# A fifth pair of row blocks by Winograd's seven products in the second GEMM of an H3 + feed-forward kernel

## The chip, the core and the metric

The kernel runs on one core of one Trainium2 chip. The metric is the device time of one execution in microseconds. TensorE (PE) multiplies matrices, VectorE (DVE) and ScalarE (ACT) work on elements, GpSimd (POOL) issues accumulating DMAs here, and SyncE (SP) issues all other DMAs from one queue, in order. Each engine runs its own instructions in the order in which they were written, and waits on semaphores for the others.

## The reference

With `xn = layernorm(q)` the output is the sum of three parts:

```
h   = silu(xn @ w1)                  # 2048 x 1024 @ 1024 x 3584
ffn = h @ w2                         # 2048 x 3584 @ 3584 x 1024
kv  = causal_conv4(k) * v
y   = long_conv(kv, ssm_k) + kv * ssm_D   # per channel, over 2048 steps
out = q + xn * y + ffn
```

All data is float32. Every matrix product is made of three fp16 matmuls (high x high, high x low, low x high), so that it keeps nearly float32's precision. To split a tile into its high and low part takes one ACT copy and one DVE subtraction.

## The kernel before, in words

**GEMM1** (`units`, `product`, `steps`) computes `h` transposed, in 14 pairs of 128 columns of `w1`. Most of it uses Winograd's form of Strassen's scheme: seven products of half-size blocks for eight. The names of the scheme are `A11, A12, A22, S1` to `S4` for sums of the left blocks and `B11, B21, B22, T1` to `T4` for those of the right; `PRODUCTS` lists the seven products P1, P7, P6, P2, P5, P3, P4 in the order in which they run. Each result goes through SiLU, is split, and is stored in DRAM: as four plain blocks a pair (`blocks`, tensor `hs`), or, for the pairs listed in `PAIRS`, as the seven left factors that GEMM2 wants (`quad`, tensors `hsf`). `quad` makes four sums on DVE (helper line 348) and seven half-size splits (lines 359 on ACT, 351 on DVE) where `blocks` makes two full-size splits for each of two row quarters.

**GEMM2** has two parts. The *plain* part (in `feed_forward`, matmuls in `steps2`, lines 1179 to 1181) runs over two halves of the output columns, 16 blocks of 128 rows and `NC` = 5 chunks of four column blocks of `h`. In the second half the last three row blocks run together, chunk by chunk, so that the places of w2's chunks come free one after the other. The *product* part (`units2`) covers the pairs in `PAIRS` (8, 9, 12, 13) for both halves at once: eight tiles, each of seven products, each product four steps of three matmuls, one step for each pair. P1 of the next tile runs between P5 and P3 of a tile. TensorE runs these in order; a step waits for its left factor (flag `h2`) and for its right factor (flag `w2f`).

**The factors of w2** are made by one generator, `norms_w2`, in a fixed order: ten plain chunks, then the seven factors in the order of `PRODUCTS`. Each waits for its place, one of eight SBUF tiles `x0` to `x7` (`places`): `W2PLACE` for the chunks, `FPLACE` for the factors. The raw blocks come from `load_w2`, which loads ahead as long as it finds a free buffer in `wraw` (two halves) or, once GEMM1 is over and two whole tiles of it are free, in `hf` (three tiles of two halves, which the evacuations use too). The sums T3, T2 and T4 build on one another and are held in place 6 (`hold`).

**The convolution** runs beside all this from about 180 us on, in eight groups of 128 channels: `gate` multiplies into the accumulator `acc` (one tile; a group's tile is free again when `signal_parts` has split all four parts of it into `cm` or `ht`), `stage1` transforms on TensorE (lines 1668 to 1670, tile `ps`), `transforms` does the rest on DVE in one chain through the tiles `spec` and `tmp`, `stage1_inv` goes back on TensorE (lines 1861 to 1863), `gated` writes `yt`, and POOL adds it to the output in DRAM. The buffers `hl` of a group's parts come free when its `stage1` is done; the next group's `gate` needs them.

**The order of the work** is written out by a planner, `Order`. Every part above is a Python generator; the planner always takes the operation that can start first by its own costs, less a bias of its stream, and emits it. So the order on each engine is fixed before the run. `yield r.ready` holds a whole generator, and everything behind it in the same generator, until the ring `r` has a free buffer.

**The last tile** of the product part doesn't add to the output by POOL but loads what is there (flag `conv out`: the convolution's last blocks for it must be on their way) and stores the sum, so its evacuation stands behind the convolution.

Of the kernel before, what the change touches and what calls it, by code (L numbers as in the profile page):

```python
# [20 lines left out]
P = 128  # L21
# [9 lines left out]
W = 512  # L31
# [20 lines left out]
RAWS = {"B11": [(0, 0)], "B21": [(1, 0)], "B22": [(1, 1)], "T1": [(0, 1), (0, 0)], "T2": [(0, 0)],  # L52
        "T3": [(1, 1), (0, 1)], "T4": [(1, 0)]}

# [241 lines left out]
def h3_ffn_kernel(ctx, tc, x, kp, vs, fs, shift, dskip, w1, w2, cfwd, cinv, out):  # L296
# [80 lines left out]
    dram = ctx.enter_context(tc.tile_pool(name="dram", bufs=1, space=bass.MemoryType.DRAM))  # L377
    hsf = [{p[0]: dram.tile([4, P, NQ, 2, P], F16, name=f"hsf{p[0]}{b}") for p in PRODUCTS.values()} for b in range(2)]
    hs = [dram.tile([4, P, NF, 2, P], F16, name=f"hs{b}") for b in range(4)]
# [528 lines left out]
    def quad(i, sp):  # L908

        def factors(names, hf, toks=()):  # L910
            n = len(names)
            yield hts.ready if n == 1 else hts.pairs
            ht, ttok = (hts.tile if n == 1 else hts.pair)([P, 4 * n, 2, P], F16, n)
            yield from split(ht[:, :, 0], ht[:, :, 1], hf, wsc[:, i, 2:3], toks)
            for f, name in enumerate(names):
                yield L(hsf[sp][name][:, :, PAIRS.index(i)].rearrange("q p h s -> p q (h s)"),
                        ht[:, 4 * f:4 * f + 4].rearrange("p q h s -> p q (h s)"))
# [216 lines left out]
    def feed_forward():  # L1134
# [12 lines left out]
        for h in range(2):  # L1147
            for ts in TOGETHER[h]:
                pos = {}
                for c in range(NC):  # L1150
                    for t in ts:
# [6 lines left out]
                        wc, wtok = w2c[h, c]  # L1158
                        yield from steps2(pos[t][0], hx, wc, c == 0, c == NC - 1)
                        htok.set()  # L1160
# [12 lines left out]

    def steps2(po, hx, wc, first, last, more=False, of=range(4), q=slice(0, W)):
        o = po[:, q]
        for n in of:
            def mm(n=n):
                kw = dict(skip_group_check=more)
                nc.tensor.matmul(o, hx[:, n, 0, :], wc[:, n, 0, q], start=first and n == 0, stop=False, **kw)  # L1179
                nc.tensor.matmul(o, hx[:, n, 0, :], wc[:, n, 1, q], start=False, stop=False, **kw)  # L1180
                nc.tensor.matmul(o, hx[:, n, 1, :], wc[:, n, 0, q], start=False, stop=last and n == 3, **kw)  # L1181
            yield T(mm, o, [hx[:, n], wc[:, n, :, q]], 3 * (size(o) / 2400 + 0.005))

# [13 lines left out]
    def units2():  # L1197

        def product2(n, u, o, first=False, of=range(4), q=slice(0, W)):
# [5 lines left out]
            if 3 not in of or q.stop < W:  # L1205
                return
            htok.set()
            if u == len(tiles2) - 1:
                wtok.set()
# [4 lines left out]
        for u in range(len(tiles2)):  # L1214
# [18 lines left out]
            if last:  # L1233
                yield from product2("P2", u, one[0], of=(0, 1))
            else:
                yield from product2("P2", u, one[0])
                made["P2"].set()
# [3 lines left out]
            if last:  # L1241
                yield from product2("P2", u, one[0], of=(2, 3))
                made["P2"].set()
# [101 lines left out]
    def load_h():  # L1345
        yield flag["factors"]
        for h in range(2):
            for c, t in [(c, t) for ts in TOGETHER[h] for c in range(NC) for t in ts]:
                yield wo.ready
                flag["h", h, t, c].what = o, _ = wo.tile([P, 4, 2, P], F16)  # L1350
                yield L(o, hs[t // 4][t % 4][:, PLAIN[4 * c]:PLAIN[4 * c] + 4])
                flag["h", h, t, c].set()
        for u, n in uses2():
            sp, q = tiles2[u]
            yield wo.ready
            flag["h2", u, n].what = o, _ = wo.tile([P, NQ, 2, P], F16)
            yield L(o, hsf[sp][PRODUCTS[n][0]][q])
            flag["h2", u, n].set()
        flag["h end"].set()

# [27 lines left out]
    def norms_w2():  # L1388
# [18 lines left out]
        for h in range(2):  # L1407
            for c in range(NC):
# [4 lines left out]
                wc, wtok = w2c[h, c] = r.tile([P, 4, 2, W], F16)  # L1413
                flag["w2", h, c].n = 2
                for a in (0, 2):
                    i = PLAIN[4 * c + a] // 2
                    raw, tok = yield from next_w2()
                    add(split(wc[:, a:a + 2, 0, :], wc[:, a:a + 2, 1, :], raw, tau[:, i:i + 1], (tok, flag["w2", h, c])), 0.05)
        yield places[FPLACE[0]].ready
        hold, ktok = places[FPLACE[0]].tile([P, NQ, W], F32)  # L1420
        for k, (name, (_, of)) in enumerate(PRODUCTS.items()):
            r = places[FPLACE[k + 1]]
            yield r.ready
            wc, wtok = w2f[name] = r.tile([P, NQ, 2, W], F16)
            flag["w2f", name].n = NQ
            held = of in ("T2", "T3", "T4")
            if held:
                if of != "T3":
                    yield flag["held", before]
                flag["held", of].n = NQ  # L1430
                before = of
            for a, i in enumerate(PAIRS):
                raw, tok = yield from next_w2()
                src, toks = raw, (tok, flag["w2f", name])
                if held:
                    src, toks = hold[:, a], (flag["w2f", name], flag["held", of])
                if of == "T3":
                    b12, t12 = yield from next_w2()
                    yield v_tt(src, raw, b12, SUB)
                    tok.set()  # L1440
                    t12.set()
                elif of == "T2":
                    yield v_tt(src, src, raw, ADD)
                    tok.set()
                elif of == "T4":
                    yield v_tt(src, raw, src, SUB)
                    tok.set()
                elif of == "T1":
                    b11, t11 = yield from next_w2()
                    yield v_tt(raw, raw, b11, SUB)  # L1450
                    t11.set()
                add(split(wc[:, a, 0, :], wc[:, a, 1, :], src, tau2[:, i:i + 1], toks), 0.05)
        yield flag["held", "T4"]
        ktok.set()

# [7 lines left out]
    def load_w2():  # L1463
# [3 lines left out]

        for h, j in [(h, j) for h in range(2) for j in PLAIN[::2]]:
            yield lambda: free("pairs")
# [3 lines left out]
        for _, of in PRODUCTS.values():  # L1473
            for i in PAIRS:
                for q, h in RAWS[of]:
                    yield lambda: free("ready")
                    raw, tok = free("ready")[0].tile([P, W])
                    yield L(raw, w2r[:, 2 * i + q, h * W:(h + 1) * W])
                    w2raw.append((raw, tok))
# [19 lines left out]
    def convolution(floor):  # L1499
# [12 lines left out]
        ps_r = py_r = ring("ps", 4, ps_c)  # L1512
        ctxs["nm"] = ps_r
        kins, kfs, accs, scs, sss, part, ipart, xgs, tmps, vals, cpart = ({} for _ in range(11))

# [17 lines left out]
        def loads():  # L1533
            for g in range(NG):
                for b in range(2):
                    yield kin_r.ready
                    kins[g, b] = kin, _ = kin_r.tile([P, T2 + HALO, P])
                    yield L(kin, kp[g, b])
                    flag["kin", g, b].set()
                    if b == 0:  # L1540
                        yield kf_r.ready
# [16 lines left out]
        def gate():  # L1558

            for g in range(NG):  # L1560
# [271 lines left out]
        def norm_rows():  # L1832

            for g in range(NG):
                for t in TO:
                    r = more["xg"]
                    yield lambda: r.ready() or flag["activations"]() and hts.ready()
                    xgs[g, t] = xg, _ = (r if r.ready() else hts).tile([P, 2, 2, P])
                    for b in range(2):
                        yield L(xg[:, b], x4[b][:, :, t, g * P:(g + 1) * P])  # L1840
# [164 lines left out]
```

## Time and profile before

| | |
|---|---|
| median of 3 runs | 1237.17 us (1236.89 to 1238.01) |
| span of the profiled execution | 1235.0 us |
| TensorE busy | 1225.7 us, 6128 matmuls |
| VectorE busy | 1121.9 us |
| ScalarE busy | 744.0 us |
| GpSimd busy | 142.0 us |
| DMA | 293.21 MB, 237 GB/s on average |
| granted TensorE clock | 0.999 |

The profiled execution's own time is its span, from the first to the last instruction; the median of the runs is 2.2 us above it. Rows of the profile read `line engine op out<-in partitions x elements xcount | busy, mean ns | idle before, releaser`. The line is that of a helper where a helper issues the operation: 348 and 351 are all two-input operations on DVE, 359 all ACT operations, 332 all loads and stores of SP. The tile names tell them apart: `x` is a place of factors, `wo` a left factor, `ff` and `ps` are PSUM. Matmul durations overlap; the time from start to start is what one costs.

### The profile page before, as it was taken

The page shows a single profiled execution, that of the slowest core. Times are in us where ns is not written, and L with a number is a line of the kernel's source. Part 1 is how long each engine was busy: PE and PEld are TensorE (multiplying, and loading weights), DVE is VectorE, ACT ScalarE, POOL GpSimd, SP SyncE. Part 2 cuts the span into 40 slices and gives each one's busy share as a digit, 9 for nine tenths or more (in the row PEclk, how much of TensorE's full clock was granted, in tenths as well). Part 3 has the DMA queues.
Part 4 walks back from the last instruction along what each step waited for, and adds up shares of the span by engine and source line. Part 5 has one row for each costly group of instructions (what it writes and reads, how often), then busy time and mean ns, then how long its engine had stood idle before and what let it go on. Part 6 is the DMA issues. An engine that isn't in the chain of part 4 may idle for free.

```text
span 1235.0 us, 17269 instructions
## 1 busy us (share of the span) xinstructions
PE 1225.7 (99%) x6128; PEld 596.6 (48%) x6128; DVE 1121.9 (91%) x1366; ACT 744.0 (60%) x1299; POOL 142.0 (12%) x164
## 2 busy tenths in 40 slices
PE   9999999999999999999999999999999999999998
PEld 7645444444444444444444544544454454445445
DVE  8999996989699979998999899989979979998993
ACT  7778887877767787758653632563263264536231
POOL 2000000000000020001110300210030030113114
PEclk9999999999999999999999999999999999999999
DMA  9289889999999698968997887699596688978777
GB/s 341 78 278 312 304 298 308 286 273 335 324 359 286 218 303 278 268 213 242 345 336 184 190 257 179 155 271 259 115 216 171 134 167 247 255 161 137 164 147 103
DMA packets 254438, 293.21 MB, mean 237 GB/s; under 512 B 48784, under 2 KB 167824, under 8 KB 252176
## 3 DMA queue, kind: packets, MB, share of 16 engines
q1 hardware_dynamic: 227760, 267.46, 69.3%
q0 software_dynamic: 26592, 24.65, 15.1%
q8 instruction: 48, 0.79, 0.3%
q14 instruction: 38, 0.31, 0.1%
HBM read 193.48 MB, written 98.57 MB: 236 GB/s over the span
## 4 chain that ended last, share of the span: by engine, by line
PE 96%; DVE 2%; ACT 1%; issue 1%; DMA 1%; POOL 0%; DVEq 0%
PE ff L1179 15%; PE ff L1180 15%; PE ff L1181 15%; PE ff L1027 13%; PE ff L1028 13%; PE ff L1029 13%; PE ps L1668 2%; PE ps L1669 2%; PE ps L1670 2%; PE ft L616 1%; PE ps L1863 1%; PE ps L1861 1%; PE ps L1862 1%; DMA out<-yt 1%; PE ff L1932 1%
## 5 line engine op out<-in xcount | busy, mean ns | idle before, releaser
L1180 PE MATMUL ff<-x,wo 128*128 128x512 f16 (+2 forms) x872 | 328.5, 377 | 0.0
L1179 PE MATMUL ff<-x,wo 128*128 128x512 f16 (+2 forms) x872 | 328.4, 377 | 0.0
L1181 PE MATMUL ff<-x,wo 128*128 128x512 f16 (+2 forms) x872 | 328.4, 377 | 0.0
L1028 PE MATMUL ff<-x,wo 128*128 128x512 f16 (+2 forms) x840 | 306.7, 367 | 1.5 <-DVE x L351 1.5
L1027 PE MATMUL ff<-x,wo 128*128 128x512 f16 (+2 forms) x840 | 306.7, 367 | 0.2 <-ACT hf L359 0.2
L1029 PE MATMUL ff<-x,wo 128*128 128x512 f16 (+2 forms) x840 | 306.7, 367 | 0.1
L348 DVE TENSOR_TENSOR spec<-spec 128x1024 f32<-128x1024 f32 (+2 forms) x272 | 263.0, 999 | 2.4
L1181 PEld LDWEIGHTS <-wo 128*128 128x128 f16 x872 | 85.3, 98 | 101.5
L1179 PEld LDWEIGHTS <-wo 128*128 128x128 f16 x872 | 85.3, 98 | 100.7
L1180 PEld LDWEIGHTS <-wo 128*128 128x128 f16 x872 | 85.3, 98 | 99.4
L1029 PEld LDWEIGHTS <-wo 128*128 128x128 f16 x840 | 82.1, 98 | 92.3 <-issue 1.6
L1027 PEld LDWEIGHTS <-wo 128*128 128x128 f16 x840 | 82.1, 98 | 88.1
L1028 PEld LDWEIGHTS <-wo 128*128 128x128 f16 x840 | 82.1, 98 | 86.9 <-issue 0.5
L345 POOL DMA_DIRECT2D out<-hf x59 | 52.5, 890 | 445.0 <-ACT hf L359 341.8
L359 ACT ACTIVATE hf<-ff,invc 128x512 f32<-128x512 f32 x60 | 41.0, 684 | 101.4 <-PE ff L1181 81.8
L345 POOL DMA_DIRECT2D out<-yt x56 | 62.0, 1278 | 326.4 <-DVE yt L351 186.7
L348 DVE TENSOR_TENSOR tmp<-spec 128x2048 f32<-128x2048 f32 (+1 forms) x48 | 92.3, 1932 | 0.9
L351 DVE SCALAR_TENSOR_TENSOR ht<-hf,wsc,ht 128x1024 f16<-128x1024 f32 (+1 forms) x56 | 67.4, 1203 | 14.5 <-ACT ht L359 14.0
L351 DVE SCALAR_TENSOR_TENSOR acc<-kin,taps,acc 128x1024 f32<-128x1024 f32 x48 | 61.4, 1278 | 7.3 <-ACT acc L359 7.3
L359 ACT ACTIVATE spec<-ps 128x512 f32<-128x512 f32 x96 | 55.4, 591 | 19.9 <-PE ps L1670 18.6
L359 ACT ACTIVATE spec<-spec 128x1024 bf16<-128x1024 f32 x32 | 33.7, 1054 | 54.9 <-DVE spec L348 54.9
L351 DVE SCALAR_TENSOR_TENSOR wo<-raw,wsc,wo 128x512 f16<-128x512 f32 (+1 forms) x56 | 56.4, 1011 | 8.3 <-ACT wo L359 8.1
(183 smaller groups left out, 1751.1 us busy)
## 6 DMA issues: line engine op xcount, KB each, us to landing
wo<-hs SPq DMA_DIRECT2D x160, 256.0 KB, 3.6
hs<-ht SPq DMA_DIRECT2D x80, 256.0 KB, 4.5
wraw<-in_w SPq DMA_DIRECT2D x31, 512.0 KB, 5.4
out<-hf POOLq DMA_DIRECT2D x59, 256.0 KB, 4.5
raw<-in_w SPq DMA_DIRECT2D x28, 512.0 KB, 5.8
kin<-in_kp SPq DMA_DIRECT2D x16, 704.0 KB, 6.2
kf<-in_fs SPq DMA_DIRECT2D x8, 1024.0 KB, 5.9
hl<-in_vs SPq DMA_DIRECT2D x32, 256.0 KB, 6.1
```

The lines of the kernel that those rows point to most:

```text
L345: return Op("POOL", 1.1, 4.8, lambda: nc.gpsimd.dma_start(o, i, accum_op=ADD), [i], [o], m, n)
L348: return V(lambda: nc.vector.tensor_tensor(o, a, b, op=op), o, [a, b], **k)
L351: return V(lambda: nc.vector.scalar_tensor_tensor(o, a, s, b, op0=op0, op1=op1), o, [a, b] + ([] if isinstance(s, float) else [s]), **k)
L359: nc.scalar.activation(o, i, func, scale=scale, **kw)
L1027: nc.tensor.matmul(o, w[:, 0, k], xf[:, :, k, 0], start=first and k == 0, stop=False, **kw)
L1028: nc.tensor.matmul(o, w[:, 0, k], xf[:, :, k, 1], start=False, stop=False, **kw)
L1029: nc.tensor.matmul(o, w[:, 1, k], xf[:, :, k, 0], start=False, stop=last and k == KH - 1, **kw)
L1179: nc.tensor.matmul(o, hx[:, n, 0, :], wc[:, n, 0, q], start=first and n == 0, stop=False, **kw)
L1180: nc.tensor.matmul(o, hx[:, n, 0, :], wc[:, n, 1, q], start=False, stop=False, **kw)
L1181: nc.tensor.matmul(o, hx[:, n, 1, :], wc[:, n, 0, q], start=False, stop=last and n == 3, **kw)
L1668: nc.tensor.matmul(o, cf[:, 0], hi[i], start=i == 0, stop=False, **kw)
L1669: nc.tensor.matmul(o, cf[:, 0], lo[i], start=False, stop=False, **kw)
```

## The change

Pair 5 joins the product part. The plain part keeps 18 column blocks, in chunks of 4, 4, 2, 4 and 4 (`CHUNKS`). A product has five steps: the four main pairs (`MAIN`) and the new one (`MORE`), which runs last.

- In GEMM1, pair 5's activations are stored by `quad`, into new tensors `hsx` that hold four and three of the seven factors together (`BATCH`). A tile loads them with two loads more (flag `h2x`).
- The right factors of the main pairs keep their form; the place for T sums (`hold`) is gone and `FPLACE` begins at place 3. The sums T3 and T2 are written to DRAM (`summed`) and read back when T2 and T4 are made. The number of raw loads for the seven factors goes from 36 to 55, with 10 stores.
- The fifth right factors live in two homes (`HOMES`): place 6 takes those of P1, P7, P6, P2, and the convolution's `acc` those of P5, P3, P4, once the last group has left it. `norms_w2` asks for a home when it comes to the first fifth factor that has none.

```diff
-PAIRS = (8, 9, 12, 13)
-NQ = len(PAIRS)
-PLAIN = [j for j in range(NF) if j // 2 not in PAIRS]
-NC = len(PLAIN) // 4
+MAIN = (8, 9, 12, 13)
+MORE = (5,)
+PAIRS = MAIN + MORE
+NM, NE, NQ = len(MAIN), len(MORE), len(PAIRS)
+CHUNKS = [(0, 4), (4, 4), (8, 2), (12, 4), (20, 4)]
+NC = len(CHUNKS)
-FPLACE = (6, 3, 4, 0, 1, 5, 2, 7)
+FPLACE = (3, 4, 0, 1, 5, 2, 7)
+HOMES = ((6, 4), ("acc", 3))
...
-RAWS = {... "T2": [(0, 0)], "T3": [(1, 1), (0, 1)], "T4": [(1, 0)]}
+RAWS = {... "T2": ["T3", (0, 0)], "T3": [(1, 1), (0, 1)], "T4": [(1, 0), "T2"]}
...
         def product2(n, u, o, first=False, of=(0, NQ), q=slice(0, W)):
+            k, f = BATCH[n]
             yield flag["h2", u, n]
             hx, htok = flag["h2", u, n].what
             yield flag["w2f", n]
             wc, wtok = w2f[n]
-            yield from steps2(o, hx, wc, first, True, not first, of, q)
+            both = [(hx[:, a], wc[:, a]) for a in range(NM)][slice(*of)]
+            end = of[1] == NQ
+            yield from steps2(o, both, first, False, not first, q)
+            if end:
+                yield flag["h2x", u, k]
+                xx, xtok = flag["h2x", u, k].what
+                yield flag["w2x", n]
+                both = [(xx[:, f, a], w2x[n][:, a]) for a in range(NE)]
+                yield from steps2(o, both, False, True, not first, q)
...
-        yield places[FPLACE[0]].ready
-        hold, ktok = places[FPLACE[0]].tile([P, NQ, W], F32)
+        homes, left = list(HOMES), []
         for k, (name, (_, of)) in enumerate(PRODUCTS.items()):
-            r = places[FPLACE[k + 1]]
+            r = places[FPLACE[k]]
             yield r.ready
-            wc, wtok = w2f[name] = r.tile([P, NQ, 2, W], F16)
+            wc, wtok = w2f[name] = r.tile([P, NM, 2, W], F16)
...
             for a, i in enumerate(PAIRS):
+                if i == MORE[0]:
+                    if not left:
+                        left = yield from home(*homes.pop(0))
+                    w2x[name] = wc = left.pop(0)
...
+                if len(RAWS[of]) > 1:
+                    other, otok = yield from next_w2()
+                    yield v_tt(raw, raw, other, ADD if of == "T2" else SUB)
+                    otok.set()
+                add(split(wc[:, a, 0, :], wc[:, a, 1, :], raw, tau2[:, i:i + 1], (tok, done)), 0.05)
+                if of in ("T3", "T2"):
+                    yield L(summed[of, i], raw)
+                    tok.set()
+                    flag["summed", of, i].set()
...
+    def home(where, n):
+        shape = [P, n, NE, 2, W]
...
+        elif where in ("kin", "acc"):
+            yield flag["last", where]
+            r = ctxs[where]
+            yield r.ready
...
+        else:
+            r = places[where]
+            yield r.ready
+            t, _ = r.tile(shape, F16)
+        return [t[:, a] for a in range(n)]
...
                 accs[g] = acc, _ = acc_r.tile([P, 2, T2, P])
+                if g == NG - 1:
+                    flag["last", "acc"].set()
```

More of the change, by code (lines that the diff above doesn't have):

```diff
@@ L1172, in h3_ffn_kernel, with steps2, mm @@
                 [(t,) for t in range(NT - 3)] + [range(NT - 3, NT)])
-    def steps2(po, hx, wc, first, last, more=False, of=range(4), q=slice(0, W)):
+    def steps2(po, both, first, last, more=False, q=slice(0, W)):
         o = po[:, q]
-        for n in of:
-            def mm(n=n):
+        for n, (hx, wc) in enumerate(both):
+            def mm(hx=hx, wc=wc, begin=first and n == 0, end=last and n == len(both) - 1):
                 kw = dict(skip_group_check=more)
[L1179 to L1182, printed above, removed]
+                nc.tensor.matmul(o, hx[:, 0, :], wc[:, 0, q], start=begin, stop=False, **kw)
+                nc.tensor.matmul(o, hx[:, 0, :], wc[:, 1, q], start=False, stop=False, **kw)
+                nc.tensor.matmul(o, hx[:, 1, :], wc[:, 0, q], start=False, stop=end, **kw)
+            yield T(mm, o, [hx, wc[:, :, q]], 3 * (size(o) / 2400 + 0.005))
     tiles2 = [(sp, q) for sp in range(2) for q in range(4)]
@@ new lines, in h3_ffn_kernel @@
+    w2x = {}
+    def home(where, n):
+        shape = [P, n, NE, 2, W]
+        if where == "hts":
+            yield lambda: flag["conv tail"]() and hts.pairs()
+            t, _ = hts.pair(shape, F16)
+        elif where in ("kin", "acc"):
+            yield flag["last", where]
+            r = ctxs[where]
+            yield r.ready
+            t, _ = r.tile([P, T2 + HALO, P] if where == "kin" else [P, 2, T2, P])
+            t = t.rearrange("p t w -> p (t w)" if where == "kin" else "p b t w -> p (b t w)")
+            t = shaped(t[:, 0:n * NE * W], shape, F16)
+        else:
+            r = places[where]
+            yield r.ready
+            t, _ = r.tile(shape, F16)
+        return [t[:, a] for a in range(n)]
@@ L1474, in load_w2 @@
             for i in PAIRS:
[L1475 removed]
+                for n, part in enumerate(RAWS[of]):
+                    if part in ("T3", "T2"):
+                        yield flag["summed", part, i]
+                        source = summed[part, i]
+                    else:
+                        source = w2r[:, 2 * i + part[0], part[1] * W:(part[1] + 1) * W]
                     yield lambda: free("ready")
[L1477 to L1478 removed]
+                    raw, tok = free("ready")[0].tile([P, W], uses=1 + (n == 0 and of in ("T3", "T2")))
+                    yield L(raw, source)
                     w2raw.append((raw, tok))
@@ L1513, in convolution @@
         ctxs["nm"] = ps_r
+        ctxs["kin"], ctxs["acc"] = kin_r, acc_r
         kins, kfs, accs, scs, sss, part, ipart, xgs, tmps, vals, cpart = ({} for _ in range(11))
@@ L1539, in loads @@
                     flag["kin", g, b].set()
+                    if (g, b) == (NG - 1, 1):
+                        flag["last", "kin"].set()
                     if b == 0:
```

83 lines of the change are left out of this document (41 added, 42 removed).

## The prediction

> **What bounds the kernel now.** I read the page's engine lines and chain of waits first.
>
> ```profile
> span 1235.0 us, 17269 instructions
> PE 1225.7 (99%) x6128; PEld 596.6 (48%) x6128; DVE 1121.9 (91%) x1366; ACT 744.0 (60%) x1299; POOL 142.0 (12%) x164
> PE 96%; DVE 2%; ACT 1%; issue 1%; DMA 1%; POOL 0%; DVEq 0%
> ```
>
> TensorE sets the end; VectorE, at 91%, is the next limit. Then the stretches of GEMM2 (first half of the columns, second half, product tiles), for all engines and then for the first of GEMM2's three matmul lines alone:
>
> ```profile
> core 0: us, PE busy (x) PEld busy (x) DVE busy (x) ACT busy (x) POOL busy (x), PEclk, DMA share, GB/s
> 825.80:1064.30 238.50, 238.50 (x1158) 112.82 (x1157) 222.97 (x253) 107.83 (x213) 32.32 (x33) 1.00 0.77 195
> 1064.30:1230.40 166.10, 166.10 (x843) 81.20 (x841) 143.87 (x161) 63.06 (x107) 45.38 (x48) 1.00 0.79 153
> ...
> 581.60:825.80 244.20, 121.26 (x320) 31.30 (x320) 1.00 0.90 239
> 825.80:1064.30 238.50, 121.26 (x320) 31.30 (x320) 1.00 0.77 195
> 1064.30:1230.40 166.10, 85.86 (x232) 22.60 (x231) 1.00 0.79 153
> ```
>
> No TensorE idle, full clock. 320 + 320 of that line are the plain chunks (16 row blocks x 2 halves x 20 column blocks); the product tiles begin at 1064.3. Times 3 lines gives 1920 plain matmuls. Inside the first product tile, counting 12 matmuls a product (P1, P7, P6, P2, P5, P1 of the next tile, P3, P4), these are the first matmuls of P1, P5 and P4:
>
> ```profile
> 1064.34 0.38 PE L1179 MATMUL ff<-x,wo 128*128 128x512 f16 x1
> ...
> 1074.70 0.38 PE L1179 MATMUL ff<-x,wo 128*128 128x512 f16 x1
> ...
> 1082.47 0.38 PE L1179 MATMUL ff<-x,wo 128*128 128x512 f16 x1
> ```
>
> 48 matmuls take 1074.70 - 1064.34 = 10.36 us: 0.2158 us each. The duration shown, 0.38, is a pipelined one.
>
> **What the change takes from TensorE.** Plain: 2 column blocks x 16 x 2 x 3 = 192 matmuls less, 41.4 us. Products: 7 x 8 tiles x 3 = 168 more, 36.3 us. Net 24 x 0.2158 = **-5.2 us**, the whole gain there is. It also moves the first product tile forward, from 1064.3 to 1064.3 - 41.4 = 1022.9. What stands still while this start moves decides the case.
>
> **The new place.** The fifth factors of P1, P7, P6 and P2 go into place 6, which is free after the first half. Those of P5, P3 and P4 go into `acc`, the convolution's accumulator, and only after its last group has been read (`acc_r.ready`; the token is set when `signal_parts` has split all four parts). The accumulator's rows for the last group, and then the last split for the group before it:
>
> ```profile
> L351 DVE SCALAR_TENSOR_TENSOR acc<-kin,taps,acc x6: 1276/1278/1279, 1016.3 to 1033.3; 128x1024 f32<-128x1024 f32 x6
> L351 DVE SCALAR_TENSOR_TENSOR cm<-acc,csc,cm x4: 735/742/747, 1048.3 to 1078.5; 128x512 f16<-128x512 f32 x4
> ...
> L351 DVE SCALAR_TENSOR_TENSOR acc<-kin,taps,acc x6: 1276/1279/1285, 917.1 to 934.6; 128x1024 f32<-128x1024 f32 x6
> L351 DVE SCALAR_TENSOR_TENSOR cm<-acc,csc,cm x4: 742/744/744, 948.9 to 971.4; 128x512 f16<-128x512 f32 x4
> ```
>
> Before, `acc` comes free at 1078.5 + 0.7 = 1079.3, when P5 of the first tile is being computed. After, TensorE reaches P5's fifth step 72 matmuls (4 products of 15, and 12) behind the tile's start: 1022.9 + 15.5 = 1038.4. At that time the last group has only just been written into `acc`. Behind the waiting matmul stand P1 of the next tile, P3, P4 and seven tiles; the evacuations and loads wait for those. Nothing else is left for TensorE except the convolution.
>
> **When is `acc` free after the change?** The release hangs on VectorE's order of work. Durations of its edits:
>
> ```profile
> L351 DVE SCALAR_TENSOR_TENSOR ht<-hf,wsc,ht 128x1024 f16<-128x1024 f32 x48 | 61.4, 1279 | 10.9 <-ACT ht L359 10.4 <-DMA kin<-in_kp 0.3
> L351 DVE SCALAR_TENSOR_TENSOR ht<-hf,wsc,ht 128x512 f16<-128x512 f32 x8 | 6.0, 747 | 3.7 <-ACT ht L359 3.6
> L351 DVE SCALAR_TENSOR_TENSOR x<-hf,tau,x 128x1024 f16<-128x1024 f32 x10 | 12.7, 1277 | 0.0
> L351 DVE SCALAR_TENSOR_TENSOR x<-x,tau,x 128x512 f16<-128x512 f32 x12 | 8.8, 742 | 0.0
> L348 DVE TENSOR_TENSOR x<-hf,x 128x512 f32<-128x512 f32 x10 | 6.8, 683 | 0.1
> ```
>
> In GEMM1 pair 5 gets seven half-size splits and four sums a half instead of two wide splits: 1.28 + 0.75 + 4 x 0.68 = 4.8 us more, twice: 9.5. In w2 it loses two wide splits (2.6) and gains seven narrow ones and four sums (5.2 + 2.7): +5.4. In all VectorE has +14.9 us.
>
> Ahead of the release stand: the quads (4.8 to 9.5; the first half's may be absorbed before the convolution starts), -2.6, the fifth elements of B11, T3, T2, B21 (0.74 + 1.43 + 1.43 + 0.74 = +4.3), and no longer B22 (4 x 0.74) and three elements of T4 (4.3): between -0.8 and +3.9. So 1078 to 1083. The other way goes by the stage-1 matmuls, whose end lets the last group begin (groups 5 and 6 here):
>
> ```profile
> L1668 PE MATMUL ps<-hl,cfw x16: 379/379/379, 878.3 to 914.6; 128*128 128x512 f16 x16
> ...
> L1668 PE MATMUL ps<-hl,cfw x16: 379/379/379, 977.5 to 1013.2; 128*128 128x512 f16 x16
> ```
>
> From that end to the release took 972.1 - 914.6 = 57.5 us and 1079.3 - 1013.2 = 66.1 us. With no delay and the shorter stretch: 1071. With 16 us of delay (the quads' 9.5, and five sums and splits of T2, 7.1, that now fall beside stage 1) and the longer: 1095. I take **1082**, nearest to the first sum. The split itself needs a sum, an ACT copy and a subtraction, about 3 us: 1085. First stall: 1085 - 1038.4 = **46.6 us** (bounds 35 and 60).
>
> **Second stall.** The generator that makes the factors waits in line for `acc`, so B22 (P3) and T4 (P4) are late too: 5 + 10 loads, two or three raw buffers in flight. Before, on VectorE (last B21; first T1, last T1, last B22, last T4):
>
> ```profile
> 1046.49 0.75 DVE L351 SCALAR_TENSOR_TENSOR x<-hf,tau,x 128x512 f16<-128x512 f32 x1
> 1048.95 0.69 DVE L348 TENSOR_TENSOR hf<-hf,wraw 128x512 f32<-128x512 f32 x1
> 1060.54 0.74 DVE L351 SCALAR_TENSOR_TENSOR x<-hf,tau,x 128x512 f16<-128x512 f32 x1
> 1067.66 0.74 DVE L351 SCALAR_TENSOR_TENSOR x<-wraw,tau,x 128x512 f16<-128x512 f32 x1
> 1082.90 0.74 DVE L351 SCALAR_TENSOR_TENSOR x<-x,tau,x 128x512 f16<-128x512 f32 x1
> ```
>
> T1 needed 8 loads in 14.1 us, 1.76 a load; T4 needed 4 loads in 15.2 us, 3.8 a load, beside the evacuations that use the same buffers. 15 loads are 26 us at the first price and 9 + 38 = 47 at the mixed one. I take 27, near the first, as few evacuations run while TensorE stands: T4's last element at 1085 + 27 = 1112. TensorE would want it 45 matmuls (9.7 us) after 1085. Second stall: **17 us** (10 to 37).
>
> **Hidden parts.** The convolution's matmuls that run inside the stalls are not run later. Before, two triples of its stage 1 fell between 1038 and 1112 (first row); the second row is how long raw loads took to land:
>
> ```profile
> L1668 PE MATMUL ps<-hl,cfw x2: 379/379/379, 1096.7 to 1097.4; 128*128 128x512 f16 x2
> ...
> DMA to landing us min/median/max: 2.8/3.9/4.8
> ```
>
> Six matmuls are 1.3 us, all 48 of a group's stage 1 are 10.4; I take **-3 us** (0 to -8). The ten stores of sums, nineteen more raw loads, sixteen small activation loads and six more GEMM1 stores lie on SP. A sum is stored a whole product before it is read, and the other loads are asked for as soon as a buffer is free, behind products of 3.2 us each. A late one would cost its landing, 3.9 us, where nothing covers it; I take 0, since the stalls cover them. VectorE's 14.9 us push the convolution's end, which a late GEMM2 covers.
>
> **Sum:** 1235.0 - 5.2 + 46.6 + 17 - 3 = 1290.4 by the profiled execution; the median of the runs is 2.2 above its span, so **1292 us**.
>
> The clock row shows 1.00 through GEMM2, with no idle stretch to test a restart. [...]
>
> **Rivals.**
>
> 1. *One stall.* `acc` comes early (1071) and the raw buffers keep up with TensorE. For it: VectorE has less GEMM work in a stall. Against it: T4's 15.2 us for four elements. 1237.2 - 5.2 + 35 = 1267, 0 to 3 less.
> 2. *Starved buffers.* Release at 1095 and the mixed price: 1237.2 - 5.2 + 60 + 37 - 5 = 1324. For it: T4's row. Against it: half of what the evacuations hold is idle in a stall.
> 3. *No stall, faster.* If P5 could have its place by 1038 the gain is whole: 1232. Against it: `acc` is still being written at 1033.3, and VectorE, 223.0 of 238.5 us busy, can't finish that group 40 us sooner. It takes that I misread the order in which the places are given.
> 4. *A tail stall instead.* With no wait for `acc`, the convolution ends later by about 10 of the 14.9 us. The last tile's evacuation waits for its output: it ended before like this (last gated block needed; load of its output).
>
> ```profile
> 1209.58 0.75 DVE L351 SCALAR_TENSOR_TENSOR wo<-ps,csc,ht 128x512 f32<-128x512 f32 x1
> ...
> 1215.88 0.33 SPq L332 DMA_DIRECT2D hf<-out  x1
> ```
>
> Then P6's copy comes at about 1221, with 13 us of products and the 4.7 us tail behind it: 1239 and 2.2, 1241. It decides from 5 us of delay on.
>
> **How the numbers follow.** Forecast 0.60 (its own range 1270 to 1315), one stall 0.15, starved 0.10, no stall 0.08, tail 0.07. The range 1252 to 1325 takes in the first three, with the bounds of the release, and leaves out about 0.18: the two without an `acc` wait and the far end of the starved one. Within 0.2% (2.5 us, what a measurement here can tell from no change) comes only by a mild tail: 0.03. Faster 0.08, slower 0.89.
>
> **What would show it.** Right: TensorE idle of 35 us or more, beginning near 1038, with VectorE's `acc` split as releaser; the last `cm<-acc` split near 1080; the `acc<-...,tau` splits right behind it; then idle pieces of a few us up to about 1112; then a dense stream of seven tiles to about 1285; the convolution over by 1225. Wrong: product tiles running through from 1023 (order of places misread); a long idle with another releaser, a DMA above all (raw loads or the DRAM sums); or a first stall of the right size and no second one (raw supply mispriced).

## The result and the profile after

The changed kernel takes 1314.82 us (median of 5, 1314.15 to 1319.91) against 1236.89 (1235.37 to 1238.01): 1.0643 times the time, interval 1.0626 to 1.0660. The prediction was 1292 with a range of 1252 to 1325. The profiled execution's span went from 1235.0 to 1313.0, which is +78.0 us.

The page of the kernel after (span, engines, two rows of the 40 slices):

```profile
span 1313.0 us, 17328 instructions
PE 1233.6 (94%) x6109; PEld 596.7 (45%) x6110; DVE 1136.3 (87%) x1387; ACT 746.8 (57%) x1308; POOL 142.2 (11%) x164
PE   9999999999999998999999999999999903799998
PEclk9999999999999999999999999999999955799999
```

One hole in TensorE's row, over three slices, and the clock at about half in it. VectorE has 14.4 us more (14.9 were predicted). The stretches around the hole, in the columns of the first windows table:

```profile
1060.00:1080.00 20.00, 0.17 (x1) 0.00 (x0) 19.83 (x20) 4.36 (x15) 0.00 (x0) 0.50 0.00 0
1080.00:1100.00 20.00, 2.72 (x6) 0.87 (x7) 19.69 (x24) 5.01 (x9) 0.00 (x0) 0.50 0.21 39
1100.00:1120.00 20.00, 9.46 (x31) 3.54 (x31) 18.58 (x25) 7.05 (x15) 0.88 (x1) 0.67 0.46 124
1120.00:1140.00 20.00, 15.34 (x76) 8.48 (x76) 16.54 (x21) 14.08 (x23) 5.28 (x5) 0.76 0.73 152
```

While TensorE does next to nothing from 1060 to 1100, VectorE is busy without a break, and it works on the convolution. Three matmuls from the timeline give the edges of the case: the first one of the first product tile, the last one before P5's fifth step, and the first one of that step, which reads `acc`:

```profile
1033.16 0.38 PE L1194 MATMUL ff<-x,wo 128*128 128x512 f16 x1
...
1051.51 0.38 PE L1196 MATMUL ff<-x,wo 128*128 128x512 f16 x1
...
1105.76 0.58 PE L1194 MATMUL ff<-acc,wo 128*128 128x512 f16 x1 [4.19 <-ACT acc L365]
```

With them the +78.0 us can be split. The prediction had the first product tile at 1022.9 and P5's fifth step 15.5 us behind it, at 1038.4; TensorE came to it at 1051.5, so it was **13.1 us** late ahead of the stall. The stall lasts from 1051.5 to 1105.8, **54.3 us**. If the matmuls save the 5.2 us that were worked out, 78.0 + 5.2 - 13.1 - 54.3 = **15.8 us** are left for what follows; this last part is a remainder and was not measured by itself.

TensorE's waits, longest groups first (engine, line, releaser, total us, times, longest):

```profile
PE ps L474 <- ACT hl L365: 19.1, 1, 19.1
PE ps L474 <- ACT spec L365: 14.0, 1, 14.0
PE ps L1721 <- DMA hl<-cm: 13.5, 1, 13.5
PE ff L1194 <- ACT acc L365: 8.2, 2, 4.2
PE ff L1041 <- DVE hf L354: 5.4, 2, 4.1
```

Only the last 4.2 us of the first stall are booked on `acc`. The planner had put eight convolution matmuls (lines 474 and 1721 to 1723) ahead of the waiting step, so the first three rows, which are pieces of the same stall, carry the releasers of those. What they wait for are steps of the convolution's last group, and VectorE works on that group until `acc` is free: from 1047.9 to 1104.3 it is busy for 55.9 of 56.4 us, with a single operation for w2. In the kernel `fifth_last` below, most of the stall is booked on `acc`.

VectorE's operations on the tile `acc` for the last group (count, duration in ns, first and last start):

```profile
L357 DVE SCALAR_TENSOR_TENSOR acc<-kin,taps,acc x6: 1276/1278/1279, 1047.9 to 1065.4; 128x1024 f32<-128x1024 f32 x6
L357 DVE SCALAR_TENSOR_TENSOR cm<-acc,csc,cm x4: 744/746/746, 1080.7 to 1103.5; 128x512 f16<-128x512 f32 x4
```

And from the timeline the right factor that TensorE waited for last, T4's fifth element:

```profile
1146.33 0.74 DVE L357 SCALAR_TENSOR_TENSOR acc<-wraw,tau,acc 128x512 f16<-128x512 f32 x1
```

The group starts at 1047.9 (before: 1016.3) and `acc` is free at 1104.3 (before: 1079.3). The mechanism is the predicted one, but everything in it comes later.

### The profile page after: what moved, and what is told of

Same layout as the page of the kernel before. It is cut to its first block, busy times and chain, and to the rows that moved or that the text cites. A ratio compares the mean times of both kernels' runs of the same rounds, so it can differ in the third digit from the quotient of the medians.

```text
span 1313.0 us, 17328 instructions
## 1 busy us (share of the span) xinstructions
PE 1233.6 (94%) x6109; PEld 596.7 (45%) x6110; DVE 1136.3 (87%) x1387; ACT 746.8 (57%) x1308; POOL 142.2 (11%) x164
## 4 chain that ended last, share of the span: by engine, by line
PE 67%; DVE 17%; issue 8%; DMA 6%; ACT 2%; POOL 1%; SPq 0%; DVEq 0%; POOLq 0%; ACTq 0%
PE ff L1195 10%; PE ff L1194 10%; PE ff L1196 10%; PE ff L1041 10%; PE ff L1042 10%; PE ff L1043 10%; DVE spec L354 6%; DVE tmp L354 3%; DMA out<-yt 2%; DMA hf<-in_w 1%; DVE ht L357 1%; PE ps L1721 1%; PE ps L1723 1%; PE ps L1722 1%; DVE acc L357 1%
## 5 line engine op out<-in xcount | busy, mean ns | idle before, releaser
L1194 PE MATMUL ff<-x,wo 128*128 128x512 f16 (+1 forms) x841 | 317.6, 378 | 1.4 <-ACT hf L365 1.1
L1195 PE MATMUL ff<-x,wo 128*128 128x512 f16 (+1 forms) x841 | 317.5, 378 | 0.0
L1196 PE MATMUL ff<-x,wo 128*128 128x512 f16 (+1 forms) x841 | 317.4, 378 | 0.0
L1041 PE MATMUL ff<-x,wo 128*128 128x512 f16 (+2 forms) x840 | 307.3, 368 | 7.4 <-DVE hf L354 5.4
L1042 PE MATMUL ff<-x,wo 128*128 128x512 f16 (+2 forms) x840 | 307.5, 368 | 1.4 <-DVE x L357 1.4
L1043 PE MATMUL ff<-x,wo 128*128 128x512 f16 (+2 forms) x840 | 307.3, 368 | 0.7 <-DVE wo L357 0.7
L351 POOL DMA_DIRECT2D out<-hf x60 | 55.5, 931 | 481.2 <-ACT hf L365 327.9
L351 POOL DMA_DIRECT2D out<-yt x60 | 68.3, 1375 | 348.1 <-DVE yt L357 200.4
L357 DVE SCALAR_TENSOR_TENSOR hf<-ff,invc,hf 128x512 f32<-128x512 f32 (+2 forms) x19 | 13.1, 692 | 74.6 <-ACT hf L365 44.9
L1721 PE MATMUL ps<-hl,cfw 128*128 128x512 f16 x120 | 46.7, 389 | 19.2 <-DMA hl<-cm 13.5
```

The lines of the kernel that those rows point to most:

```text
L351: return Op("POOL", 1.1, 4.8, lambda: nc.gpsimd.dma_start(o, i, accum_op=ADD), [i], [o], m, n)
L357: return V(lambda: nc.vector.scalar_tensor_tensor(o, a, s, b, op0=op0, op1=op1), o, [a, b] + ([] if isinstance(s, float) else [s]), **k)
L1041: nc.tensor.matmul(o, w[:, 0, k], xf[:, :, k, 0], start=first and k == 0, stop=False, **kw)
L1042: nc.tensor.matmul(o, w[:, 0, k], xf[:, :, k, 1], start=False, stop=False, **kw)
L1043: nc.tensor.matmul(o, w[:, 1, k], xf[:, :, k, 0], start=False, stop=last and k == KH - 1, **kw)
L1194: nc.tensor.matmul(o, hx[:, 0, :], wc[:, 0, q], start=begin, stop=False, **kw)
```

## The experiments

**1. Another home (`wo_home`).** The fifth factors of P5, P3 and P4 go into three reserved halves of the ring of left factors.

```diff
-HOMES = ((6, 4), ("acc", 3))
+HOMES = ((6, 4), ("wo", 1), ("wo", 1), ("wo", 1))
...
```

> The changed kernel, but the fifth factors of P5, P3 and P4 go into three halves of wo, the ring of left factors, in place of acc; nothing waits for the convolution's last group. Theory (the wait for acc makes both stalls): the 52.7 us lost between 1051 and 1106 and nearly all of the 18 us lost behind it go; what stays is the 14 us lost before that and the convolution's later end: 1240 to 1252 us. Rival A (the 14.9 us of added VectorE work set the end and the wait is only where it shows): TensorE stands somewhere else instead, at least half of the loss stays, 1275 us or more. Rival B (raw loads and sums through DRAM come late): idle pieces of 10 us or more in front of P6 or P4 with a DMA or the sum as releaser, 1260 to 1300 us.

1266.59 us, 1.0232 (1.0217 to 1.0247): 48 us less than the changed kernel, and the first stall is gone. But it isn't within the 1240 to 1252 expected. One stretch, in the columns of the windows table:

```profile
1066.00:1084.00 18.00, 6.50 (x17) 1.81 (x16) 18.00 (x21) 7.67 (x19) 0.87 (x1) 0.60 0.56 163
```

One wait in it, and VectorE's sum ahead of it, from the timeline:

```profile
1066.48 0.38 PE L1196 MATMUL ff<-x,wo 128*128 128x512 f16 x1
1071.80 0.58 PE L1194 MATMUL ff<-x,wo 128*128 128x512 f16 x1 [4.94 <-ACT x L365]
...
1070.30 0.69 DVE L354 TENSOR_TENSOR wraw<-wraw 128x512 f32<-128x512 f32 x1
```

In 18 us TensorE does 6.5 us of work, in pieces between the steps of P4, which wait for elements of T4 (the sum at 1070.30 is the one for which the step at 1071.80 waits). The wait for `acc` is shown as the cause of the first stall; the second one doesn't need `acc`.

**2. More raw buffers (`wo_raw2`).** As 1, and two more halves of `wo` hold raw blocks of w2 from the product part on.

```diff
+        for _ in range(2):
+            yield wo.ready
+            spare_raw.append([wo.tile([P, W])[0], None])
...
-            return [r for r in (ctxs["wraw"], hfs)[:1 + rest] if getattr(r, kind)()]
+            return [r for r in (ctxs["wraw"], spares, hfs)[:2 + rest] if getattr(r, kind)()]
```

> The kernel with the fifth factors of P5, P3 and P4 in halves of `wo`, and two more halves of `wo` as raw buffers of w2 from the product part on (30 of the 35 halves are left for left factors). Theory (the 16.2 us that TensorE lost between 1066 and 1084 there are raw blocks that came late for want of buffers, half clock included): that loss is gone, 1266.6 - 16 = 1250, between 1246 and 1257; what is left above before are the early losses of GEMM1 (12 to 14 us) and the convolution's delay. Rival A (the way of the T sums through DRAM is what is late, so that more buffers do nothing): 1262 to 1268, with stops at P4's steps as before. Rival B (the left factors' loads now starve, as `wo` has fewer halves): stops with a `wo` load as releaser, 1258 or more.

1252.63 us, 1.0117 (1.0102 to 1.0133). The same 18 us, and the stretch ahead of it:

```profile
1055.00:1066.00 11.00, 6.87 (x28) 2.68 (x27) 8.58 (x11) 3.92 (x8) 2.62 (x4) 0.92 1.09 267
1066.00:1084.00 18.00, 18.00 (x81) 7.96 (x79) 16.74 (x17) 8.78 (x19) 1.88 (x3) 0.95 0.82 214
```

TensorE is busy through the 18 us. The T sums still go through DRAM here, so their way was not the cause: raw blocks came late for want of a buffer. A smaller stop is new, 3.4 us before 1063.6, for a left factor (`wo<-hsfA`). SyncE's queue shows how it came about:

```profile
1051.13 0.32 SPq L338 DMA_DIRECT2D wo<-sumT  x1
1058.76 0.55 SPq L338 DMA_DIRECT2D ht<-in_x  x1
1059.39 0.56 SPq L338 DMA_DIRECT2D wo<-hsfA  x1
```

The load was issued 0.7 us before TensorE needed it and landed 4.1 us after its issue (the median of such loads is 3.3 in this run), so it was asked for too late. It stands behind a load into `ht`, and the queue waited 7.0 us before that one, by the profile for the transfer `out<-ht` that still read the buffer.

**3. The quads alone (`quad_alone`).** The kernel before, with pair 5 stored as seven left factors as well; GEMM2 keeps four pairs, and its third plain chunk reads the left blocks of the second, so that part of the output is left out.

```diff
+QUADS = PAIRS + (5,)
...
-        if i in PAIRS:
+        if i in QUADS:
             return
```

> The kernel before, with one part of the change alone: pair 5's activations are stored as seven left factors in GEMM1, as in the change. GEMM2 is as before, except that its third chunk reads the left blocks of the second one, so the output lacks pairs 4 and 5's own product there. Theory (the quads' 9.5 us of VectorE work make the 14 us of early TensorE loss and most of the convolution's delay, which is 10 us at group 0 and 32 us at group 7): TensorE idle of 8 to 14 us before 590 us, group 0's gate starts 8 to 11 us later than 216, 1244 to 1256 us. Rival (the early losses come from the reshuffled order of the whole plan, not from the quads): less than 4 us of idle before 590 us, 1236 to 1241 us.

1251.13 us, 1.0114 (1.0093 to 1.0136): some 14 us slower (1249.4 for 1235.0 by the spans), though TensorE has the same matmuls. The first line of GEMM1's matmuls in the costliest groups (before, it had no idle of this kind: 0.2 us):

```profile
L1030 PE MATMUL ff<-x,wo 128*128 128x512 f16 (+2 forms) x840 | 307.3, 368 | 6.8 <-DVE hf L349 5.4
```

The last group on VectorE, by the tile `acc`:

```profile
L352 DVE SCALAR_TENSOR_TENSOR acc<-kin,taps,acc x6: 1277/1280/1280, 1035.7 to 1055.8; 128x1024 f32<-128x1024 f32 x6
```

And the first matmul of the first product tile:

```profile
1074.36 0.38 PE L1182 MATMUL ff<-x,wo 128*128 128x512 f16 x1
```

GEMM1's PSUM evacuations stand behind the quads' work on VectorE, the first product tile starts 10.0 us later than before (1064.34), and the last group 19.4 us later. The 9.5 us of VectorE work that the prediction covered with other work are here paid in full before GEMM2's products begin; the rest of the 14 us comes behind that.

**4. The last group first (`gate_first`).** The changed kernel, with one wait more.

```diff
+            if name == "P6":
+                yield flag["last", "acc"]
             r = places[FPLACE[k]]
```

> The changed kernel, but the generator of w2's factors waits before P6's factor until the convolution's last group has been given `acc`. Between the sixth and the seventh start of the `acc` products VectorE had 21 operations of w2's factors in the changed kernel (15.3 us) and none before. Theory (these, moved forward with the first product tile, delayed the last group by some 15 us of the 31.6; the quads made the rest): the last group starts at 1030 to 1038 for 1047.9, and the last `cm` split of `acc` comes 10 to 15 us earlier than 1104.3; P6's and later factors come late in turn, so that the time is no better, 1312 to 1324. Rival A (the last group is late for its loads or for stage 1's matmuls, not for VectorE): it starts at 1045 or later all the same. Rival B (the release moves as said and the factors are made in time beside it): 1298 to 1306.

1312.39 us (a single time). What VectorE does for w2 in the changed kernel between the starts of groups 6 and 7, counted from 0, in the `acc` products (931.9 to 1047.9), by groups; in the kernel before the same gap has no such row:

```profile
L357 DVE SCALAR_TENSOR_TENSOR x<-hf,tau,x 128x512 f16<-128x512 f32 x10 | 7.4, 745 | 0.0
L354 DVE TENSOR_TENSOR hf<-hf,wraw 128x512 f32<-128x512 f32 x5 | 3.4, 683 | 0.0
L357 DVE SCALAR_TENSOR_TENSOR x<-wraw,tau,x 128x512 f16<-128x512 f32 x4 | 2.9, 745 | 0.0
...
```

With four more sums of 0.7 us each, these are 23 operations, 16.5 us (the expectation had counted 21). The gap grew from 99.2 us (917.1 to 1016.3) to 116.0, by 16.8. With the wait, in `gate_first`:

```profile
L357 DVE SCALAR_TENSOR_TENSOR acc<-kin,taps,acc x6: 1276/1278/1279, 1029.6 to 1055.2; 128x1024 f32<-128x1024 f32 x6
...
L357 DVE SCALAR_TENSOR_TENSOR cm<-acc,csc,cm x4: 745/746/746, 1072.8 to 1095.9; 128x512 f16<-128x512 f32 x4
```

The group starts 18.3 us sooner. The release comes only 7.6 us sooner (10 to 15 were expected), since the factors that were held back now stand ahead of it: between the start of the last group and its release VectorE does 19 operations for w2, 13.5 us, where the changed kernel has one. The time doesn't improve, as far as a single run can tell: the work was moved about on the same full engine.

**5. The order of the factors (`fifth_last`).** The main factors of P5, P3 and P4 are made first, the three fifth ones at the end.

```diff
+ORDER2 = [(n, "all") for n in ("P1", "P7", "P6", "P2")]
+ORDER2 += [(n, "main") for n in ("P5", "P3", "P4")] + [(n, "fifth") for n in ("P5", "P3", "P4")]
...
```

> The changed kernel, but w2's factors come in another order: the four main ones of P5, P3, P4 first, then the three fifth ones, which alone wait for acc. Theory (the second stall comes from the factors that stand in line behind the wait): P5's fifth step still waits to about 1105, but P3 and P4 follow with less than 6 us of loss in place of 18: 1293 to 1303 us. Rival (the second stall is slow raw loads or the half-rate clock, whatever the line): 1309 us or more.

1303.87 us (a single time), a little over the upper edge. TensorE's longest waits:

```profile
PE ff L1196 <- ACT acc L367: 34.3, 1, 34.3
PE ps L476 <- ACT hl L367: 20.7, 1, 20.7
```

The 20 us behind the release, in the columns of the windows table:

```profile
1108.00:1128.00 20.00, 18.41 (x79) 7.94 (x79) 19.83 (x27) 5.45 (x14) 2.60 (x3) 0.88 0.60 141
```

The first stall stays, and 34.3 us of it now have `acc` as releaser; the idle pieces behind it are nearly gone. The kernel is 11 us faster although `acc` came free 2.7 us later here (1107.0 for 1104.3), so the place of the fifth factors in the generator's line makes most of the 15.8 us.

**6. A home that is free sooner (`kin_home`).** P5 and P3's fifth factors in the convolution's `kin`, P4's in `acc`.

```diff
-HOMES = ((6, 4), ("acc", 3))
+HOMES = ((6, 4), ("kin", 2), ("acc", 1))
```

> The changed kernel, but the fifth factors of P5 and P3 go into kin, the convolution's input tile, last read at about 1066 in the profile of the changed kernel, and only P4's into acc. Theory (the time follows the release of the place): P5's fifth step runs at about 1070 in place of 1106, P4's fifth step waits for acc until about 1105, and P3's and P4's main factors are made meanwhile: 1278 to 1295 us. Rival (the added VectorE work sets it): 1308 us or more.

1297.18 us (a single time), 2 us above the range. TensorE waits 16.4 us for `kin` at P5's fifth step, but the steps behind wait for elements of the factors and then for `acc`. Its waits:

```profile
PE ff L1194 <- ACT kin L365: 18.9, 2, 16.4
PE ff L1194 <- ACT x L365: 10.5, 3, 5.8
PE ff L1194 <- ACT acc L365: 5.8, 1, 5.8
```

**7. Warm through the stall (`warm`).** Contrary to what its expectation says of the result, the repeated passes add into the same sum, so P5's four main steps count eighteen times in the first tile; only the time is read.

```diff
+AGAIN = 17
...
+            if (u, n) == (0, "P5"):
+                for _ in range(AGAIN):
+                    yield from steps2(o, both, first, False, not first, q)
```

> The changed kernel, but TensorE repeats the first four steps of the first tile's P5 seventeen more times before it goes on (17 x 12 matmuls of 0.216 us, 44 us, the last pass counts, so the result is the same). The first stall is filled with matmuls, and the clock stays up to the release of `acc`. Theory (T4's raw blocks, not the clock, set when the dense stream begins again): 1312 to 1317, no change to the changed kernel's 1314.8, with the idle pieces behind the release a little longer. Rival A (half clock after the stall costs on the path: the 15 matmuls at 0.426 between 1105.8 and 1112.2 and those up to 1129): 1306 to 1311. Rival B (the convolution's matmuls between are held up behind the repeated ones and `acc` comes later): 1318 or more.

1316.01 us, 1.0630 (1.0616 to 1.0645). The stretch of the stall and the next, in the columns of the windows table:

```profile
1051.00:1098.00 47.00, 47.00 (x219) 21.26 (x218) 46.55 (x50) 13.73 (x33) 0.88 (x1) 1.00 0.22 51
1098.00:1120.00 22.00, 9.86 (x32) 3.69 (x31) 21.35 (x28) 6.57 (x14) 0.88 (x1) 0.69 0.42 107
```

VectorE's fifth splits into `acc` (the last start is P4's):

```profile
L358 DVE SCALAR_TENSOR_TENSOR acc<-wraw,tau,acc x2: 746/746/747, 1107.6 to 1147.8; 128x512 f16<-128x512 f32 x2
```

Full clock and a full TensorE up to 1098, and the end is no sooner: T4's last split starts at 1147.8 for 1146.3, and all behind it with it. The half clock inside the first stall (0.53 in the changed kernel from 1051 to 1098) cost nothing. The extra matmuls ended 7 us too early for the release, and the clock fell again behind them (0.69 from 1098 to 1120), so what a warm restart at the release is worth wasn't tried.

**8. Another pair (`wo_raw3_p7`).** As 2 with three raw halves, and pair 7 in place of pair 5.

```diff
-MORE = (5,)
+MORE = (7,)
...
-CHUNKS = [(0, 4), (4, 4), (8, 2), (12, 4), (20, 4)]
+CHUNKS = [(0, 2), (2, 4), (6, 4), (10, 4), (20, 4)]
```

> The same with three raw halves of `wo` and pair 7 in place of pair 5 as the fifth pair, chunks of 2, 4, 4, 4 and 4. Theory (the early losses are pair 5's quads meeting the convolution's first groups, and come from the place of the quads in GEMM1, not from their mere number): the stops near 428 and 517 us go or shrink to under 5 us in all, and the time falls to 1236 to 1244. Rival A (seven products for eight in GEMM1's activations cost VectorE the same wherever they fall): early losses of 12 us again, 1246 to 1256. Rival B (the convolution's delay, not TensorE's stops, sets the end now): stops gone, but a wait of the last tile for the convolution's output, 1244 to 1252.

1240.46 us, 1.0020 (1.0010 to 1.0030). The stops near 428 and 517 are gone and one near 234 is there:

```profile
L1041 PE MATMUL ff<-x,wo 128*128 128x512 f16 (+2 forms) x840 | 307.3, 368 | 2.9 <-DVE hf L354 2.9
```

The third raw half plays no part there, as it is used from the product part on. So with the same number of quads their place in VectorE's work makes a difference. They also cost at a distance: in the changed kernel pair 5's second quad stores its factors (`hsx`) from 413.9 to 432.1, where the stop near 428 is, but the longer stop at 517 is at a quad of a main pair (`hsf`, 508.0 to 523.2).

**9 to 11. Near it.** `wo_raw4_p7` has one raw half more than 8, `wo_raw4_p3` the same with pair 3 and chunks to fit, `wo_raw3_p7_bias` is 8 with the planner's bias of the factors at 0.06.

```diff
-        for _ in range(3):
+        for _ in range(4):
...
-(norms_w2(), 0.03)
+(norms_w2(), 0.06)
```

> The kernel with pair 7 in place of pair 5, three halves of `wo` for fifth factors, and four for raw blocks in place of three. Theory (what is left there, 1.6 + 3.2 us and their half clock between 1035 and 1057, are left factors that land 6.7 us after their issue among raw loads of w2, so one more raw buffer doesn't help): 1238 to 1243. Rival A (raw blocks are still short): that loss is gone, 1234 to 1237. Rival B (too few halves of `wo` are left for left factors): 1245 to 1256.

> The same with pair 3 as the fifth pair, chunks of 4, 2, 4, 4 and 4. Theory (VectorE's added work is the same wherever it falls, what differs is whether a quad meets a row of evacuations): stops of 3 to 6 us near a quad of pair 3, at another time than 234 us; 1238 to 1246. Rival (quads that fall earlier, ahead of most of the convolution, cost nothing): 1233 to 1237.

> Pair 7 with three raw halves, and the planner's bias of w2's factors raised from 0.03 to 0.06, so that factors are made a little sooner against the convolution. Theory (the convolution and TensorE both have slack of a few us by now): within 3 us of 1240.5. Rival (the stops at 1035 to 1057 come from the order on VectorE): 1234 to 1237.

In this order: 1246.85 us, 1.0076 (1.0063 to 1.0089), in the range of the rival that too few halves are left for left factors, though no wait is shown for it; 1241.46, 1.0035 (1.0023 to 1.0047); 1240.25, 1.0017 (1.0008 to 1.0026). None beats the kernel before. In `wo_raw3_p7_bias` the 5.2 us of saved matmuls are lost again in small stops, 2.9 us for the evacuations (`hf`) in GEMM1 and 2.2 us for ScalarE's `spec` in GEMM2 among them, and in matmuls 0.43 us apart behind the second (the last section has its rows).

## Why the prediction came out as it did

The time fell into the range 23 us above the forecast. The mechanism of the stalls was right; one term stood at nothing and shouldn't have, and two sizes were off. By the spans, the 22.6 us between 1290.4 and 1313.0 are 13.1 of late arrival, 7.7 of a longer first stall and 1.8 behind it. No term of the sum and no rival holds the 13.1: that the range took them in is luck.

**-5.2 us of matmuls**: 19 fewer are on record (24 by the program; some records are missing), and in a full stretch they keep 0.216 us from start to start.

**VectorE's 14.9 us at nothing** is the step that failed. Their size was right (14.4). The cover was wrong: I had let "a late GEMM2" hide them, but 9.5 of them fall in GEMM1, where TensorE waits for its evacuations on VectorE, long before anything is late. The row of the waits shows it (5.4 us for `hf`), and `quad_alone`, with the same stops near 428 and 517, shows the cause and a price: its first product tile is 10.0 us late. In the changed kernel that tile starts 10.3 us behind the predicted 1022.9. The other 2.8 of the 13.1 us arose inside the tile, in six convolution matmuls (1.3 us) and two waits for evacuations, none of which stood in the prediction's 15.5. The line that should have warned me stood in the prediction: VectorE at 91%.

**The release at 1082, bounds 1071 to 1095**: it came at 1104.3, outside the bounds. The last group starts 31.6 us later, 1047.9 for 1016.3. 14.8 us of it are there already at group 6 (931.9 for 917.1). `quad_alone` has 19.4 at the last group, all of it there at group 6 (the gap between them is 99.3 us, as before), where I had 4.8 to 9.5 for the quads. The other 16.8 arise between groups 6 and 7, where 16.5 us of factors of w2 now stand; `gate_first` holds them back and the group starts 18.3 us sooner. My worst case had five sums and splits of T2 there (7.1 us); with the first product tile, B21's five splits and four sums and splits of T1 had moved forward too. Since arrival and release were late together, the stall was mis-sized by less, 54.3 for 46.6.

**The second stall, 17 - 3**: 15.8 us in all. The line behind `acc` was right (`fifth_last`). T4's last element was there 41.3 us after the first step that reads `acc` (1105.8 and 1146.33 + 0.74), where I took 27, near the low price; it was nearer the high bound, 47. Little of that shows in the time, because the convolution's matmuls ran in the waits: TensorE is busy for 15.3 of the 20 us from 1120 to 1140. Between 1105.8 and 1147.1 the product needs 45 matmuls, 9.7 us, and 87 of the convolution ran beside them, worth 13.7 us at full rate, where I had taken 3 as hidden. Two errors of the opposite sign met, and that the sum of this term came out near is luck. `wo_home` and `wo_raw2` show that the raw buffers, which the prediction has only in the price of a load, are a limit of their own: 14 us without any wait for `acc`.

**The DRAM sums at nothing** holds as far as `wo_raw2` can show: with two more raw buffers the sums go the same way, and TensorE is busy through the stretch that had waited for T4.

**The restart at half clock**: behind the first stall twelve matmuls take 4.65 us from 1107.53 to 1112.18, for 2.59 at full rate, so 2.1 us go there (the granted clock was 0.50 from 1105.8 to 1112.2). But T4's last element is ready at 1147.07 and its step starts at 1147.16, so no part of them is shown to reach the end.

**Rivals.** *One stall* and *no stall* are refuted. *Starved buffers* came nearer than the forecast, 1324 in all, by its late release and its mixed raw price, which was about right; but it counts 60 and 37 us for the two stalls, where 54.3 and 15.8 were seen, and has nothing for GEMM1. The *tail stall* has no room in this kernel: the last matmul starts 3.8 us before the end of the span, before 4.7.

**What would show it**: the idle began at 1051.5 for 1038, the last `cm` split came at 1103.5 for 1080, the dense stream ended at 1309 for 1285; the splits into `acc` stood right behind the release, as said. Most of the idle was booked on the convolution's matmuls, with ScalarE and a DMA as releasers. Another releaser was to be a sign of being wrong; the trace alone doesn't settle that, `wo_home` does.

## What to carry to other kernels

A saving on the bound engine moves the stage behind it forward, and with it the deadlines of all side work: list what the side engine must now do before the *new* time, in order, and not only what the edit adds. An engine that is 91% busy off the critical path gives no cover that may be taken for granted: look for the places where the bound engine waits for it, since what added work costs hangs on where it falls (some 14 us with pair 5's quads, with pair 7's a stop of 2.9 us in GEMM1 and, for 3.0 us behind it, matmuls 0.43 us apart in place of 0.22). A buffer lent from another stage costs the wait for its last reader and everything queued behind the request in the same stream.

## What the hardware showed

Behind a wait of 4.13 us TensorE's granted clock was 0.53 for 3.65 us, and 1.00 after that. In the changed kernel, around the stop at 517:

```profile
517.11 0.38 PE L1043 MATMUL ff<-x,wo 128*128 128x512 f16 x1
521.62 0.55 PE L1041 MATMUL ff<-x,wo 128*128 128x512 f16 x1 [4.13 <-DVE hf L354]
521.97 0.63 PE L1042 MATMUL ff<-x,wo 128*128 128x512 f16 x1
...
525.25 0.38 PE L1041 MATMUL ff<-x,wo 128*128 128x512 f16 x1
```

Nine matmuls start in the 3.63 us from 521.62 to 525.25, most of them 0.43 us apart, where full rate would need 1.94: 1.7 us are lost. In `wo_raw3_p7_bias` the like stands behind less idle:

```profile
1026.15 0.38 PE L1196 MATMUL ff<-x,wo 128*128 128x512 f16 x1
1028.77 0.38 PE L1751 MATMUL ps<-hl,cfw 128*128 128x512 f16 x1 [2.24 <-ACT spec L365]
...
1029.85 0.59 PE L1196 MATMUL ff<-x,wo 128*128 128x512 f16 x1
1030.23 0.63 PE L1194 MATMUL ff<-x,wo 128*128 128x512 f16 x1
...
1033.48 0.38 PE L1196 MATMUL ff<-x,wo 128*128 128x512 f16 x1
```

The idle was 2.24 us, and the first five matmuls behind it started 0.22 us apart; from 1029.85 on, 1.1 us after the work had begun again, nine took 3.63 us, most of them 0.43 us apart. In `wo_home` the clock was 0.95 from 1023 to 1060, where TensorE stood for 2.7 of the 37 us. In `wo_raw4_p3` an idle of 2.32 us at 1043 was followed by full clock (1.00 from 1040 to 1060). What tells them apart no run here shows.
